# A post-norm residual block on one core: x loaded in three pieces, LayerNorm statistics taken for four row groups at a time, and another route for the last output

## The chip, the core and the metric

The kernel runs on one core of a Trainium2 chip. The metric is the device time of one execution in microseconds. Before the change it is 26.49 us, the median of six runs (26.14 to 26.74). The profile below is of one execution; the span from its first to its last instruction is 24.9 us, some 1.6 us less than the device time, because the device time also holds what comes ahead of the first instruction and after the last.

## The reference

```python
# x: (4, 256, 256) fp32, i.e. 1024 rows of 256; w_block: (256, 256); gamma: (256,)
h = np.maximum(x @ w_block, 0.0)
y = x + h
mu = y.mean(-1, keepdims=True)
sigma = np.sqrt(y.var(-1, keepdims=True) + 1e-6)
return ((y - mu) / sigma * gamma).astype(np.float32)
```

The 1024 rows lie on 128 partitions. A partition holds eight rows, and the kernel works on two of them at once: a "pair" is a tile of 128 partitions x 2 rows x 256 columns, and there are four pairs, numbered 0 to 3 here. Pairs 0 and 1 are the first half of x, pairs 2 and 3 the second. What the changed kernel calls a quad is two pairs, so four row groups.

## The kernel before

Loads first: `w` and `gamma` come over ScalarE's DMA queue in fp32 and are cast to bf16 on chip. x comes over GpSimd's queue, which casts it to bf16 on the way, in two loads of two pairs each.

```python
    w_stage = const.tile([P, KC, D], FP32)
    nc.scalar.dma_start(out=w_stage, in_=w_block.rearrange("(kc p) n -> p kc n", p=P))
    w_sb = const.tile([P, KC, D], BF16)
    nc.scalar.copy(out=w_sb, in_=w_stage)
    # ... gamma_stage in the same way, cast by VectorE; eps_sb; make_identity(nc, ident)
    x_sb = []
    for h in range(NH):                                     # NH = 2
        t_ = xp.tile([P, G, D], BF16, name=f"x_sb{h}", tag=f"x{h}")   # G = 4 rows
        nc.gpsimd.dma_start(out=t_, in_=x_v[h])
        x_sb.append(t_)
```

Then one loop over the four pairs. TensorE transposes x, ScalarE copies the transposed tile out of PSUM, TensorE multiplies by w, ScalarE applies relu, VectorE adds x and takes mean and variance; ScalarE and VectorE make 1/sigma; VectorE normalises; GpSimd multiplies by gamma and writes fp32; SyncE's queue sends the tile out.

```python
    for pr in range(n_pairs):                               # 4 pairs
        # ... 4 transposes of x into pxt (PSUM)
        nc.scalar.copy(out=xt_sb, in_=pxt)                          # L89
        # ... 4 matmuls of xt_sb with w_sb into ph (PSUM)           # L94
        nc.scalar.activation(out=relu_h, in_=ph, func=AF.Relu)      # L103
        nc.vector.tensor_tensor(out=y, in0=x_sb[h][:, f0:f0+PAIR, :], in1=relu_h, op=ALU.add)  # L106
        for t in range(PAIR):
            nc.vector.bn_stats(out=bn6[:, t, :], in_=y[:, t, :])    # L113
            nc.vector.bn_aggr(out=mv[:, t, :], in_=bn6[:, t, :])    # L114
        nc.scalar.activation(out=std, in_=mv[:, :, 1], func=AF.Sqrt, bias=eps_sb)   # L117
        nc.vector.reciprocal(out=rstd, in_=std)                     # L119
        for t in range(PAIR):
            nc.vector.tensor_scalar(tq[:, t, :], in0=y[:, t, :], scalar1=mv[:, t, 0:1],
                scalar2=rstd[:, t:t+1], op0=ALU.subtract, op1=ALU.mult)             # L123
        nc.gpsimd.tensor_tensor(out=o, in0=tq,
            in1=gamma_sb.to_broadcast([P, PAIR, D]), op=ALU.mult)   # L133, fp32 out
        nc.sync.dma_start(out=out_v[h][:, f0:f0+PAIR, :], in_=o)    # L137
```

A scheduler decides in which order the instructions of different pairs stand on an engine, so that order is not the loop's.

Of the kernel before, what the change touches and what calls it, by code (L numbers as in the profile page):

```python
# [1 line left out]

# [6 lines left out]

FP32 = mybir.dt.float32
BF16 = mybir.dt.bfloat16
AF = mybir.ActivationFunctionType
ALU = mybir.AluOpType
AX = mybir.AxisListType


@with_exitstack
def kernel(
    ctx: ExitStack,  # L20
    tc: tile.TileContext,
    x: bass.AP,
    w_block: bass.AP,
    gamma: bass.AP,
    out: bass.AP,
):
    nc = tc.nc
    P = 128

    x_flat = x.flatten_outer_dims()  # L30
    out_flat = out.flatten_outer_dims()
    N, D = x_flat.shape
    assert D == 256 and N == 1024
    KC = D // P
    G = 4
    NH = N // (P * G)
    PAIR = 2
    n_pairs = N // (P * PAIR)

    eps = 1e-6  # L40

    x_v = x_flat.rearrange("(h q f) d -> h q f d", q=P, f=G)
    out_v = out_flat.rearrange("(h q f) d -> h q f d", q=P, f=G)

    const = ctx.enter_context(tc.tile_pool(name="const", bufs=1))
    xp = ctx.enter_context(tc.tile_pool(name="xp", bufs=2))
    xtp = ctx.enter_context(tc.tile_pool(name="xtp", bufs=3))
    hp = ctx.enter_context(tc.tile_pool(name="hp", bufs=3))
    yp = ctx.enter_context(tc.tile_pool(name="yp", bufs=3))
    op_ = ctx.enter_context(tc.tile_pool(name="op", bufs=3))  # L50
    stat = ctx.enter_context(tc.tile_pool(name="stat", bufs=4))
    ps_xt = ctx.enter_context(tc.tile_pool(name="ps_xt", bufs=2, space=bass.MemoryType.PSUM))
    ps_h = ctx.enter_context(tc.tile_pool(name="ps_h", bufs=4, space=bass.MemoryType.PSUM))

    w_stage = const.tile([P, KC, D], FP32)
    nc.scalar.dma_start(out=w_stage, in_=w_block.rearrange("(kc p) n -> p kc n", p=P))
    w_sb = const.tile([P, KC, D], BF16)
    nc.scalar.copy(out=w_sb, in_=w_stage)  # L58

    gamma_stage = const.tile([P, 1, D], FP32)  # L60
    nc.scalar.dma_start(out=gamma_stage, in_=gamma.partition_broadcast(P))
    gamma_sb = const.tile([P, 1, D], BF16)
    nc.vector.tensor_copy(out=gamma_sb, in_=gamma_stage)  # L63

    eps_sb = const.tile([P, 1], FP32)
    nc.vector.memset(eps_sb, eps)

    ident = const.tile([P, P], BF16)
    make_identity(nc, ident)

    x_sb = []
    for h in range(NH):
        t_ = xp.tile([P, G, D], BF16, name=f"x_sb{h}", tag=f"x{h}")
        nc.gpsimd.dma_start(out=t_, in_=x_v[h])  # L74
        x_sb.append(t_)

    for pr in range(n_pairs):
        h = (pr * PAIR) // G
        f0 = (pr * PAIR) % G

        pxt = ps_xt.tile([P, PAIR, KC, P], BF16)
        for t in range(PAIR):
            for c in range(KC):
                nc.tensor.transpose(  # L84
                    pxt[:, t, c, :], x_sb[h][:, f0 + t, ts(c, P)], ident
                )

        xt_sb = xtp.tile([P, PAIR, KC, P], BF16)
        nc.scalar.copy(out=xt_sb, in_=pxt)  # L89

        ph = ps_h.tile([P, PAIR, D], FP32)
        for t in range(PAIR):
            for c in range(KC):
                nc.tensor.matmul(  # L94
                    ph[:, t, :],
                    lhsT=xt_sb[:, t, c, :],
                    rhs=w_sb[:, c, :],
                    start=(c == 0),
                    stop=(c == KC - 1),
                )  # L100

        relu_h = hp.tile([P, PAIR, D], BF16)
        nc.scalar.activation(out=relu_h, in_=ph, func=AF.Relu)  # L103

        y = yp.tile([P, PAIR, D], BF16)
        nc.vector.tensor_tensor(  # L106
            out=y, in0=x_sb[h][:, f0 : f0 + PAIR, :], in1=relu_h, op=ALU.add
        )

        bn6 = stat.tile([P, PAIR, 6], FP32)  # L110
        mv = stat.tile([P, PAIR, 2], FP32)
        for t in range(PAIR):
            nc.vector.bn_stats(out=bn6[:, t, :], in_=y[:, t, :])  # L113
            nc.vector.bn_aggr(out=mv[:, t, :], in_=bn6[:, t, :])  # L114

        std = stat.tile([P, PAIR], FP32)
        nc.scalar.activation(out=std, in_=mv[:, :, 1], func=AF.Sqrt, bias=eps_sb)  # L117
        rstd = stat.tile([P, PAIR], FP32)
        nc.vector.reciprocal(out=rstd, in_=std)  # L119

        tq = op_.tile([P, PAIR, D], BF16)
        for t in range(PAIR):
            nc.vector.tensor_scalar(  # L123
                tq[:, t, :],
                in0=y[:, t, :],
                scalar1=mv[:, t, 0:1],
                scalar2=rstd[:, t : t + 1],
                op0=ALU.subtract,
                op1=ALU.mult,
            )  # L130

        o = op_.tile([P, PAIR, D], FP32, tag="out")
        nc.gpsimd.tensor_tensor(  # L133
            out=o, in0=tq, in1=gamma_sb.to_broadcast([P, PAIR, D]), op=ALU.mult
        )

        nc.sync.dma_start(out=out_v[h][:, f0 : f0 + PAIR, :], in_=o)  # L137


# [1 line left out]
_INS = ['x', 'w_block', 'gamma']  # L141
_OUTS = [((4, 256, 256), 'float32')]


# [23 lines left out]
```

## Time and profile before

| what | value |
| --- | --- |
| device time, median of 6 | 26.49 us (26.14 to 26.74) |
| span of the profiled execution | 24.9 us |
| VectorE (DVE) busy | 9.4 us, 38% of the span |
| ScalarE (ACT) busy | 8.5 us, 34% |
| GpSimd (POOL) busy | 6.6 us, 27% |
| TensorE (PE) busy | 4.9 us, 20% |
| first x load, issue to landing | 6.2 us |
| second x load, issue to landing | 6.4 us |
| an output store of 256 KB, issue to landing | 2.0 us |

No engine is busy for even half of the span, so the shares do not say what bounds the kernel; the order of events does. The table of engine timelines gives, for each instruction or run of equal instructions, when it starts and how long it takes, counted from the first instruction. The chain of waits follows the work that ended last back to what released it. A tile name with a number, such as x_sb_97, is the program's: x_sb_97 is the first x load and x_sb_99 the second.

### The profile page before, as it was taken

The page shows a single profiled execution, that of the slowest core. Times are in us where ns is not written, and L with a number is a line of the kernel's source. Part 1 is how long each engine was busy: PE and PEld are TensorE (multiplying, and loading weights), DVE is VectorE, ACT ScalarE, POOL GpSimd, SP SyncE. Part 2 cuts the span into 40 slices and gives each one's busy share as a digit, 9 for nine tenths or more (in the row PEclk, how much of TensorE's full clock was granted, in tenths as well). Part 3 has the DMA queues.
Part 4 walks back from the last instruction along what each step waited for, and adds up shares of the span by engine and source line. Part 5 has one row for each costly group of instructions (what it writes and reads, how often), then busy time and mean ns, then how long its engine had stood idle before and what let it go on. Part 6 is the DMA issues. An engine that isn't in the chain of part 4 may idle for free.

```text
span 24.9 us, 182 instructions
## 1 busy us (share of the span) xinstructions
PE 4.9 (20%) x32; PEld 3.4 (14%) x32; DVE 9.4 (38%) x34; ACT 8.5 (34%) x15; POOL 6.6 (27%) x12
## 2 busy tenths in 40 slices
PE   0000000000009699995970000000000000000000
PEld 0000000000009267690730000000000000000000
DVE  0000000000400000199960699999998992000000
ACT  0029836000000971789999991000053000000000
POOL 3398500000000000000000029708901975930000
PEclk9999999999999999999999998555555555555555
DMA  0006997999954000000000000007305500822800
GB/s 0 0 13 115 345 72 58 118 140 204 204 102 89 13 0 0 0 0 0 0 0 0 0 0 0 0 0 293 128 0 224 197 0 0 332 89 109 313 0 0
DMA packets 1280, 1.97 MB, mean 79 GB/s; under 512 B 128, under 2 KB 512, under 8 KB 1280
## 3 DMA queue, kind: packets, MB, share of 16 engines
q0 software_dynamic: 288, 0.52, 12.3%
q1 hardware_dynamic: 576, 1.05, 11.2%
q10 hardware_dynamic: 416, 0.39, 10.5%
HBM read 1.44 MB, written 1.05 MB: 100 GB/s over the span
## 4 chain that ended last, share of the span: by engine, by line
DVE 26%; DMA 25%; ACT 12%; PE 10%; issue 7%; POOLq 5%; POOL 1%; DVEq 0%
DMA x_sb_97<-in_x_dram 25%; DVE tq L123 11%; PE ph L94 8%; ACT xt_sb L89 6%; DVE y L106 6%; POOLq L163 5%; ACT L117 3%; DVE bn_181 L113 3%; DVE bn_213 L113 3%; PE pxt L84 2%; ACT relu_h L103 2%; DVE rstd L119 2%; DVE mv L114 2%; ACT std L117 1%; POOL ident masks.py:197 1%
## 5 line engine op out<-in xcount | busy, mean ns | idle before, releaser
L133 POOL TENSOR_TENSOR o<-tq,gamma_sb 128x512 f32<-128x512 bf16 x4 | 4.7, 1176 | 14.4 <-DVE tq L123 12.8
L89 ACT COPY xt_sb<-pxt 128x512 bf16<-128x512 bf16 x4 | 2.1, 590 | 4.0 <-PE pxt L84 4.0
L123 DVE TENSOR_SCALAR tq<-y,mv,rstd 128x256 bf16<-128x256 bf16 x8 | 3.2, 435 | 0.1
L94 PE MATMUL ph<-w_sb,xt_sb 128*128 128x256 bf16 x16 | 3.0, 350 | 0.6 <-ACT xt_sb L89 0.6
L103 ACT ACTIVATE relu_h<-ph 128x512 bf16<-128x512 f32 x4 | 2.3, 590 | 0.9 <-PE ph L94 0.9
L84 PE MATMUL pxt<-ident,x_sb_97 128*128 128x128 bf16 x8 | 1.0, 311 | 7.5 <-DMA x_sb_97<-in_x_dram 7.5
L106 DVE TENSOR_TENSOR y<-x_sb_97,relu_h 128x512 bf16<-128x512 bf16 x2 | 0.8, 410 | 4.0 <-ACT relu_h L103 4.0
L63 DVE CAST gamma_sb<-gamma_stage 128x256 bf16<-128x256 f32 x1 | 0.3, 293 | 5.4 <-DMA gamma_stage<-in_gamma_dram 5.4
L117 ACT ACTIVATE std<-mv,eps_sb 128x2 f32<-128x2 f32 x4 | 1.2, 294 | 3.3 <-DVE mv L114 3.3
L94 PEld LDWEIGHTS <-xt_sb 128*128 128x128 bf16 x16 | 1.7, 121 | 1.6 <-ACT xt_sb L89 1.1
L58 ACT ACT_TABLE_LOAD x1 | 1.3, 1283 | 1.7 <-PEq L152 1.7
L84 PEld LDWEIGHTS <-x_sb_97 128*128 128x128 bf16 x8 | 0.8, 141 | 7.5 <-DMA x_sb_97<-in_x_dram 7.5
L106 DVE TENSOR_TENSOR y<-x_sb_99,relu_h 128x512 bf16<-128x512 bf16 x2 | 1.6, 804 | 0.0
L117 ACT ACT_TABLE_LOAD x1 | 1.3, 1283 | 0.0
L84 PE MATMUL pxt<-ident,x_sb_99 128*128 128x128 bf16 x8 | 1.1, 314 | 0.0
L119 DVE RECIPROCAL rstd<-std 128x2 f32<-128x2 f32 x4 | 0.7, 164 | 1.0 <-ACT std L117 1.0
L84 PEld LDWEIGHTS <-x_sb_99 128*128 128x128 bf16 x8 | 0.9, 151 | 0.1
L74 POOL DMA_DIRECT2D x_sb_97<-in_x_dram x1 | 0.7, 717 | 0.3 <-issue 0.3
L58 ACT CAST w_sb<-w_stage 128x512 bf16<-128x512 f32 x1 | 0.6, 617 | 0.5 <-DMA w_stage<-in_w_block_dram 0.5
L113 DVE BATCH_NORM_STATS2 bn_213<-y 128x6 f32<-128x256 bf16 x2 | 0.8, 390 | 0.0
L113 DVE BATCH_NORM_STATS2 bn_117<-y 128x6 f32<-128x256 bf16 x2 | 0.8, 418 | 0.0
L113 DVE BATCH_NORM_STATS2 bn_149<-y 128x6 f32<-128x256 bf16 x2 | 0.8, 418 | 0.0
(13 smaller groups left out, 3.5 us busy)
## 6 DMA issues: line engine op xcount, KB each, us to landing
out_dram<-o SPq DMA_DIRECT2D x4, 256.0 KB, 2.0
w_stage<-in_w_block_dram ACTq DMA_DIRECT2D x1, 256.0 KB, 2.8
x_sb_97<-in_x_dram POOLq DMA_DIRECT2D x1, 256.0 KB, 6.2
x_sb_99<-in_x_dram POOLq DMA_DIRECT2D x1, 256.0 KB, 6.4
gamma_stage<-in_gamma_dram ACTq DMA_DIRECT2D x1, 128.0 KB, 5.0
```

The lines of the kernel that those rows point to most:

```text
L58: nc.scalar.copy(out=w_sb, in_=w_stage)
L84: nc.tensor.transpose(pxt[:, t, c, :], x_sb[h][:, f0 + t, ts(c, P)], ident)
L89: nc.scalar.copy(out=xt_sb, in_=pxt)
L94: nc.tensor.matmul(ph[:, t, :], lhsT=xt_sb[:, t, c, :], rhs=w_sb[:, c, :], start=(c == 0), stop=(c == KC - 1),)
L103: nc.scalar.activation(out=relu_h, in_=ph, func=AF.Relu)
L106: nc.vector.tensor_tensor(out=y, in0=x_sb[h][:, f0 : f0 + PAIR, :], in1=relu_h, op=ALU.add)
L113: nc.vector.bn_stats(out=bn6[:, t, :], in_=y[:, t, :])
L117: nc.scalar.activation(out=std, in_=mv[:, :, 1], func=AF.Sqrt, bias=eps_sb)
L119: nc.vector.reciprocal(out=rstd, in_=std)
L123: nc.vector.tensor_scalar(tq[:, t, :], in0=y[:, t, :], scalar1=mv[:, t, 0:1], scalar2=rstd[:, t : t + 1], op0=ALU.subtract, op1=ALU.mult,)
L133: nc.gpsimd.tensor_tensor(out=o, in0=tq, in1=gamma_sb.to_broadcast([P, PAIR, D]), op=ALU.mult)
L163: with _tile.TileContext(nc) as tc:
```

## The change

Three things are done, each for a reason that the program text gives.

- x is loaded in three pieces instead of two, pair 0 alone, pair 1 alone, and pairs 2 and 3 together, so that pair 0 need not wait for pair 1's data. The identity and the x loads also stand ahead of the w and gamma loads in the program text.
- The square root and the reciprocal are taken once for two pairs (128x4 values) instead of once for each pair (128x2).
- The last pair's multiplication by gamma moves from GpSimd to VectorE and writes bf16; its store then goes over GpSimd's queue, which casts to fp32 on the way. The other three pairs keep the old route.

```diff
+    x_load_slices = [(0, 0, PAIR), (0, PAIR, G), (1, 0, G)]
+    for li, (h, fs, fe) in enumerate(x_load_slices):
+        t_ = xp.tile([P, fe - fs, D], BF16, name=f"x{li}", tag=f"x{li}")
+        nc.gpsimd.dma_start(out=t_, in_=x_v[h][:, fs:fe, :])
...
-    for h in range(NH):
-        t_ = xp.tile([P, G, D], BF16, name=f"x_sb{h}", tag=f"x{h}")
-        nc.gpsimd.dma_start(out=t_, in_=x_v[h])
...
-    for pr in range(n_pairs):
+    for qd in range(n_pairs // QUAD):
+        ys = []
+        for pq in range(QUAD):
...          (transposes, copy, matmuls, relu, y, bn_stats, bn_aggr as before)
+        nc.scalar.activation(out=std, in_=mv[:, :, 1], func=AF.Sqrt, bias=eps_sb)
+        nc.vector.reciprocal(out=rstd, in_=std)
+        for pq in range(QUAD):
...          (two tensor_scalar for the pair as before)
+            if not last:
+                nc.gpsimd.tensor_tensor(out=o, in0=tq, in1=gamma_sb.to_broadcast([P, PAIR, D]), op=ALU.mult)
+                nc.sync.dma_start(out=out_v[h][:, f0 : f0 + PAIR, :], in_=o)
+            else:
+                ob = op_.tile([P, PAIR, D], BF16, tag="out_bf16")
+                nc.vector.tensor_tensor(out=ob, in0=tq, in1=gamma_sb.to_broadcast([P, PAIR, D]), op=ALU.mult)
+                nc.gpsimd.dma_start(out=out_v[h][:, f0 : f0 + PAIR, :], in_=ob)
```

## The prediction

> **What bounds the kernel now.** I read the chain of waits first. It runs from the first x load through the first pair's TensorE and ScalarE work to VectorE, stays there from 13.9 us, and ends with GpSimd's last product and its store. So I then read each engine's timeline. First the start, in the page's list of costliest groups (engine, output and inputs, count; busy and mean ns; idle time before and what ended it) and its list of transfers:
>
> ```profile
> L84 PE MATMUL pxt<-ident,x_sb_97 128*128 128x128 bf16 x8 | 1.0, 311 | 7.5 <-DMA x_sb_97<-in_x_dram 7.5
> x_sb_97<-in_x_dram POOLq DMA_DIRECT2D x1, 256.0 KB, 6.2
> gamma_stage<-in_gamma_dram ACTq DMA_DIRECT2D x1, 128.0 KB, 5.0
> ```
>
> Nothing computes before 7.49 us. Next ScalarE's timeline (start, us, what):
>
> ```profile
> 9.85 0.60 ACT L103 ACTIVATE relu_h<-ph 128x512 bf16<-128x512 f32 x1 [0.64 <-PE ph L94]
> 10.71 0.60 ACT L103 ACTIVATE relu_h<-ph 128x512 bf16<-128x512 f32 x1 [0.26 <-PE ph L94]
> 11.20 1.07 ACT L89 COPY xt_sb<-pxt 128x512 bf16<-128x512 bf16 x2
> 12.29 1.28 ACT L117 ACT_TABLE_LOAD   x1
> 13.58 0.29 ACT L117 ACTIVATE std<-mv,eps_sb 128x2 f32<-128x2 f32 x1
> ```
>
> The first std ends at 13.88 because ScalarE runs four copies, two relus and a table load before it; VectorE waits 1.03 us for it. After that VectorE never rests for long. Its timeline and GpSimd's, around two places:
>
> ```profile
> 14.80 1.25 POOL L133 TENSOR_TENSOR o<-tq,gamma_sb 128x512 f32<-128x512 bf16 x1 [11.94 <-DVE tq L123]
> 15.15 1.19 DVE L106 TENSOR_TENSOR y<-x_sb_99,relu_h 128x512 bf16<-128x512 bf16 x1
> ...
> 19.23 1.15 POOL L133 TENSOR_TENSOR o<-tq,gamma_sb 128x512 f32<-128x512 bf16 x1 [1.15 <-DVE rstd L119]
> 19.33 1.39 DVE L123 TENSOR_SCALAR tq<-y,mv,rstd 128x256 bf16<-128x256 bf16 x2
> 20.85 1.15 POOL L133 TENSOR_TENSOR o<-tq,gamma_sb 128x512 f32<-128x512 bf16 x1 [0.47 <-POOL o L133]
> ```
>
> An addition that takes 0.42 us elsewhere takes 1.19 here, and ends 0.29 after GpSimd's product (16.05). Two normalisations that take 0.58 take 1.39; the first alone takes 1.13. So GpSimd's product holds VectorE off, twice, for about 0.8 us each. At the end: product 20.85 to 22.00, store issued at 22.0, landed 2.0 us later at 24.0, and 0.9 us of closing work to 24.9. The bound is a chain of latencies: load, ScalarE's six operations and table load, VectorE with two blockings, store.
>
> **What the Trainium skill says.** "SBUF — State Buffer", section "Who interferes with whom": VectorE in a two-port mode, or with two SBUF inputs, and a GpSimd operation that reads SBUF exclude each other for a whole instruction. The trace agrees (1.19 and 1.13 us above); bn_stats, with one input, ran beside GpSimd's second product in its usual 0.39 to 0.42 us. "ScalarE: Activation LUTs", section "What ACT_TABLE_LOAD costs": about 1283 ns; the trace has 1283. "DMA: Bandwidth & Descriptors", section "SWDGE vs HWDGE vs iDMA": a casting transfer must come from GpSimd, where software writes the descriptors. The trace has 0.72 and 0.56 us of GpSimd time for the two x issues, and 0.33 to 0.37 on SyncE's queue for a store.
>
> **Part 1, the x load.** Of the 6.2 us little is x's own: its queue's packets are 12.3% of the span, 3.06 us for both loads, 1.53 each, so 0.77 for one pair. The rest is contention and latency. The DMA row (slices of 0.62 us) gives 345 GB/s in slice 4, which is w, then 72, 58, 118, 140, then 204 twice, which is x alone. Summing the row, 0.54 MB have moved by 5.6 us; w (0.26) and gamma (0.13) are in it, so about 0.14 MB of x, just above one pair (0.13 MB as bf16). Pair 0 could thus have its data at 5.5 to 5.9 us (its packets are half as large and share turns with gamma's). The old load had its 0.26 MB, by the same sum, at about 6.2 and landed at 7.45, 1.25 later, some of that being slow engines. With 0.8 to 1.2 us for the shorter one, pair 0 lands at about **6.65**, a gain of 0.8 (0.3 to 1.1). The split adds one GpSimd issue (0.56) behind it, so pairs 2 and 3 still land near the old 8.7 to 9.2.
>
> **Part 2, ScalarE up to the first std.** The order of instructions in the built program has changed. Before: copy, copy, relu, relu, copy, copy, table load, std. Now: copy 0, relu 0, copies 1 and 2, relus 1 and 2, copy 3, table load, std. One relu more (0.5) stands ahead of the table load, and TensorE now multiplies pair 0 before it transposes pair 1, so copy 1 comes after relu 0. With the durations of the trace: transposes 6.70 to 7.32 (four took 0.62), copy 0 to 7.93, four matmuls to 9.05 (1.05 from 8.78 to 9.83 before), relu 0 to 9.67, copies 1 and 2 to 10.77, matmuls 1 to about 10.95, relu 1 to 11.6, matmuls 2 and relu 2 to 12.3, copy 3 to 12.8, table load to 14.1, std to **14.35**. That is 0.5 us later than the old 13.88: the gain of part 1 is eaten in this order. In exchange VectorE has by then done pair 2's addition and statistics too (0.42 + 0.74), which it did after the first std before.
>
> **Part 3, VectorE from the first std to the last store.** Removed: two of four std (0.29 each, mostly hidden) and two of four reciprocals (0.17 each). Remaining serial work, from the trace's durations: reciprocal and two aggregations 0.25, four normalisations 1.08, addition 0.4, two bn_stats and aggregations 0.95, std with handover 0.35, reciprocal 0.2, four normalisations 1.1, product in bf16 0.43 (as the addition of the same shape): 4.8 us. GpSimd's three products (1.15 each) exclude normalisations and additions. One fits beside bn_stats, aggregation, std and reciprocal (1.5 us in all); the other two hold VectorE off by about 1.1 each. Depending on whether GpSimd gets between two normalisations or only after them, blocking sums to 1.8 to 2.3. So the last bf16 product ends 6.6 to 7.1 us after the first std; with 6.9, at 21.2. The old kernel issued its last store at 22.0.
>
> **Part 4, the last store.** It now costs GpSimd 0.56 to 0.72 us of descriptors, where the old store's data started to move about 0.85 us after its issue. Data: 0.77 us, as for one pair of x. Receipt as before, about 0.4. I take 2.5 us to landing against 2.0, an estimate. So 21.2 + 2.5 = 23.7, and with the same 0.9 of closing a span of 24.6: 0.3 less than 24.9, of which product and store together give about 0.3 (1.28 of GpSimd replaced by 0.43 + 0.08, minus 0.5 for the slower route). Device time 26.49 - 0.3 = 26.2; I leave 0.1 for the third load's extra traffic and say **26.3**.
>
> **Rivals.**
> - ScalarE's order does not cost what I say: TensorE is warm early and std ends by 13.6. For it: the later transposes ran at about 0.13 us each, the first at 0.155. Against: the copies and relus are fixed at 0.59. This would give 25.5.
> - The x load gains nothing, because gamma's slow packets (5.0 us to landing) hold the smaller packets of pair 0 as well. Then std comes at 15.1 and the time is 27.1. For it: 72 and 58 GB/s while the DMA engines are nine and seven tenths busy.
> - GpSimd's store is much slower than 2.5 us. The only such transfers in the trace took 6.2 and 6.4, though in a crowd. At 3.3 us the time is 27.0.
> - GpSimd's product becomes the bound: pairs 0 and 1 are normalised together, so their products queue (2.3 us), and the last store must stand behind the third product on GpSimd. If all three run back to back without gaps it is still 3.5 us after about 15.2, so 18.7, which is before 20.5. It delays by blocking, not by its own length. Unlikely to cost over 0.4.
>
> **Range and chances.** I take errors of about 0.4 us for the x load, 0.4 for the store, 0.5 for the blocking and 0.3 for ScalarE's order; as independent errors they make 0.8 us. Eight in ten is then about 25.3 to 27.2. Two per cent of 26.49 is 0.53, so the borders are 25.96 and 27.02. From 26.3 they lie 0.4 and 0.9 of such an error away: about one third below, a fifth above, the rest between.
>
> **What would show it.** The first transposes at 6.7 (right from 6.4 to 7.2); the first 128x4 std ending near 14.35, behind seven ScalarE operations and the table load; a normalisation or addition of over 1 us beside the first product and another beside the third; the bf16 product at about 0.43; the store landing 2.5 us after issue. I am wrong above all if the first transposes move by under 0.3, if no VectorE operation is held off beside GpSimd, or if the store takes over 3 us.

## The result, and the profile after

The changed kernel takes 25.85 us (median of ten, 25.5 to 26.37), the kernel before 26.51 us in the executions beside it. The ratio is 0.972, with a 95% interval of 0.967 to 0.978: faster by nearly three per cent. The ratios here and below leave out disturbed executions; the medians hold all. The span of the profiled execution is 24.0 us instead of 24.9. The old profile is of an execution of 26.68 us, a little above the median, so spans differ by 0.9 and times by 0.66.

The start first, from the page of the changed kernel: a group of instructions (with what ended the idle time before it), then two transfers with the time from issue to landing in the last column.

```profile
L103 PE MATMUL pxt<-ident,x_87 128*128 128x128 bf16 x4 | 0.6, 308 | 5.3 <-DMA x_87<-in_x_dram 5.3
...
gamma_stage<-in_gamma_dram ACTq DMA_DIRECT2D x1, 128.0 KB, 3.4
x_87<-in_x_dram POOLq DMA_DIRECT2D x1, 128.0 KB, 4.0
```

TensorE starts at 5.30 us, not 7.49: pair 0 is there 2.2 us sooner (other profiles with the old loads have 7.04 to 7.50). Gamma, whose load nobody touched, landed after 3.4 us instead of 5.0. Now ScalarE's timeline up to the first std (start, us, what, idle before it):

```profile
7.66 0.60 ACT L120 ACTIVATE relu_h<-ph 128x512 bf16<-128x512 f32 x1 [1.13 <-PE ph L111]
...
9.86 0.60 ACT L120 ACTIVATE relu_h<-ph 128x512 bf16<-128x512 f32 x1 [0.64 <-PE ph L111]
10.93 0.60 ACT L120 ACTIVATE relu_h<-ph 128x512 bf16<-128x512 f32 x1 [0.47 <-PE ph L111]
11.42 0.58 ACT L106 COPY xt_sb<-pxt 128x512 bf16<-128x512 bf16 x1
12.02 1.28 ACT L131 ACT_TABLE_LOAD   x1
13.31 0.30 ACT L131 ACTIVATE std<-mv,eps_sb 128x4 f32<-128x4 f32 x1
```

The first std ends at 13.61, only 0.27 sooner than the old 13.88. Of the 2.2 us 1.9 are spent again on the way there. Relu 2 now stands ahead of the table load (0.6 us), and the relus ahead of it wait 2.2 us for TensorE in all (the idle times above) instead of 0.9 (0.64 and 0.26 in the old timeline). Next VectorE's timeline from there to the end:

```profile
13.87 1.93 DVE L144 TENSOR_SCALAR tq<-y,mv,rstd 128x256 bf16<-128x256 bf16 x4
15.72 0.41 DVE L123 TENSOR_TENSOR y<-x_91,relu_h 128x512 bf16<-128x512 bf16 x1
16.17 0.75 DVE L128 BATCH_NORM_STATS2 bn_161<-y 128x6 f32<-128x256 bf16 x2
...
17.72 1.95 DVE L144 TENSOR_SCALAR tq<-y,mv,rstd 128x256 bf16<-128x256 bf16 x4
19.70 0.43 DVE L161 TENSOR_TENSOR ob<-tq,gamma_sb 128x512 bf16<-128x512 bf16 x1
```

and GpSimd's:

```profile
14.54 1.18 POOL L155 TENSOR_TENSOR o<-tq,gamma_sb 128x512 f32<-128x512 bf16 x1 [11.19 <-DVE tq L144]
15.88 1.26 POOL L155 TENSOR_TENSOR o<-tq,gamma_sb 128x512 f32<-128x512 bf16 x1 [0.16 <-DVE tq L144]
18.40 1.18 POOL L155 TENSOR_TENSOR o<-tq,gamma_sb 128x512 f32<-128x512 bf16 x1 [1.25 <-DVE tq L144]
20.42 0.60 POOL L164 DMA_DIRECT2D out_dram<-ob  x1 [0.84 <-DVE ob L161]
```

Four normalisations take 1.93 us where two pairs of 0.58 would take some 1.1, and each time a GpSimd product starts in the middle of them. GpSimd's second product, at 15.88, runs beside the addition and the statistics, which take their usual time. The last product ends at 20.13, the casting store begins at 20.42, lands 2.3 later at 22.7, and the span ends at 24.0.

So the 0.9 us of span come from these differences. The first std is 0.27 sooner. From the end of that std to the end of the last product there are 6.52 us instead of 8.12 (13.88 to 22.00): 1.6 less, above all because pair 2's addition and statistics (0.42 + 0.74) are already done and because the last product takes 0.43 instead of 1.15. Handover and store cost 2.6 us instead of 2.0, and the closing, from the last landing to the end of the span, 1.3 instead of 0.9: one microsecond given back.

The identity and the x loads also moved up in the program text. The issues did not move with them: the first x load is issued at 1.25 us and w's at 0.74 in both profiles.

### The profile page after: what moved, and what is told of

Its sections match the earlier page's. It is cut to its first block, busy times and chain, and to the rows that moved or that the text cites. A ratio compares the mean times of both kernels' runs of the same rounds, so it can differ in the third digit from the quotient of the medians.

```text
span 24.0 us, 180 instructions
## 1 busy us (share of the span) xinstructions
PE 5.8 (24%) x32; PEld 3.7 (15%) x32; DVE 10.1 (42%) x33; ACT 8.1 (34%) x13; POOL 6.6 (28%) x13
## 4 chain that ended last, share of the span: by engine, by line
ACT 18%; DVE 17%; DMA 17%; PE 16%; issue 9%; POOL 6%; POOLq 3%
DMA x_87<-in_x_dram 17%; PE ph L111 12%; DVE tq L144 10%; ACT xt_sb L106 7%; POOL o L155 5%; ACT L131 5%; PE pxt L103 3%; ACT relu_h L120 3%; DVE bn_161 L128 3%; POOLq L190 3%; ACT std L131 3%; DVE rstd L132 2%; DVE mv L129 2%; DVE y L123 1%; POOL ident masks.py:197 1%
## 5 line engine op out<-in xcount | busy, mean ns | idle before, releaser
L155 POOL TENSOR_TENSOR o<-tq,gamma_sb 128x512 f32<-128x512 bf16 x3 | 3.6, 1208 | 12.6 <-DVE tq L144 12.6
L111 PE MATMUL ph<-w_sb,xt_sb 128*128 128x256 bf16 x16 | 4.2, 416 | 1.9 <-ACT xt_sb L106 1.9
L144 DVE TENSOR_SCALAR tq<-y,mv,rstd 128x256 bf16<-128x256 bf16 x8 | 3.9, 549 | 0.0
L123 DVE TENSOR_TENSOR y<-x_87,relu_h 128x512 bf16<-128x512 bf16 x1 | 0.4, 426 | 3.4 <-ACT relu_h L120 3.4
L131 ACT ACTIVATE std<-mv,eps_sb 128x4 f32<-128x4 f32 x2 | 0.6, 298 | 3.1 <-DVE mv L129 3.1
L128 DVE BATCH_NORM_STATS2 bn_103<-y 128x6 f32<-128x256 bf16 x4 | 1.5, 418 | 0.1
L128 DVE BATCH_NORM_STATS2 bn_161<-y 128x6 f32<-128x256 bf16 x4 | 1.5, 418 | 0.0
L164 POOL DMA_DIRECT2D out_dram<-ob x1 | 0.6, 602 | 0.8 <-DVE ob L161 0.8
L123 DVE TENSOR_TENSOR y<-x_91,relu_h 128x512 bf16<-128x512 bf16 x2 | 0.8, 402 | 0.0
```

The costliest lines, as they stand in the source:

```text
L111: nc.tensor.matmul(ph[:, t, :], lhsT=xt_sb[:, t, c, :], rhs=w_sb[:, c, :], start=(c == 0), stop=(c == KC - 1),)
L123: nc.vector.tensor_tensor(out=y, in0=xs, in1=relu_h, op=ALU.add)
L128: nc.vector.bn_stats(out=bn6[:, g, :], in_=y[:, t, :])
L155: nc.gpsimd.tensor_tensor(out=o, in0=tq, in1=gamma_sb.to_broadcast([P, PAIR, D]), op=ALU.mult)
```

## The experiments

**Each part alone, and all but the split.**

The split alone, on the old kernel:

```diff
-    for h in range(NH):
-        t_ = xp.tile([P, G, D], BF16, ...); nc.gpsimd.dma_start(out=t_, in_=x_v[h])
+    for li, (h, fs, fe) in enumerate([(0, 0, PAIR), (0, PAIR, G), (1, 0, G)]):
+        t_ = xp.tile([P, fe - fs, D], BF16, ...); nc.gpsimd.dma_start(out=t_, in_=x_v[h][:, fs:fe, :])
...          (x_pairs names the tile and rows of each pair)
```

> The old kernel with the load of x in three pieces and nothing else. Theory A: the smaller first load lands near 5.3 us, as in the changed kernel, and in the order that results two copies, one relu fewer stand ahead of the first std than in the changed kernel (copy 0, relu 0, copies 1 and 2, relu 1, table load, std), so the first std ends near 12 us instead of 13.88 and the time falls by 1 to 1.8 us, to about 25. Rival B: the early landing in the changed kernel's profile was chance of that execution (gamma, which was not changed, also landed 1.6 us sooner), so the first load lands near 6.65 and the time is 25.8 to 26.3.

Measured: 26.01 us against 26.42, ratio 0.981 (0.975 to 0.988). The first transposes begin at 5.38, so the early landing was no chance. ScalarE's and VectorE's timelines in this run:

```profile
10.55 1.28 ACT L118 ACT_TABLE_LOAD   x1
11.85 0.30 ACT L118 ACTIVATE std<-mv,eps_sb 128x2 f32<-128x2 f32 x1
...
12.26 0.41 DVE L114 BATCH_NORM_STATS2 bn<-y 128x6 f32<-128x256 bf16 x1
...
13.18 0.39 DVE L114 BATCH_NORM_STATS2 bn<-y 128x6 f32<-128x256 bf16 x1
...
19.16 0.17 DVE L120 RECIPROCAL rstd<-std 128x2 f32<-128x2 f32 x1 [0.36 <-ACT std L118]
```

The first std ends at 12.15, as theory A said, 1.7 us sooner than in the old kernel. But the time fell by 0.4, not by 1 to 1.8. My step from "first std" to "end" was wrong: VectorE still has pair 1's two bn_stats to take after the std (0.41 and 0.39), which it used to take before it, and it waits 0.36 us for the last std. Here the earlier std only exchanges waiting on VectorE before it for work after it.

The tail alone, on the old kernel:

```diff
+        if pr == n_pairs - 1:
+            nc.vector.tensor_tensor(out=ob, in0=tq, in1=gamma..., op=ALU.mult)     # ob is bf16
+            nc.gpsimd.dma_start(out=out_v[h][:, f0 : f0 + PAIR, :], in_=ob)
+        else: ...  # product on GpSimd in fp32, store from SyncE's queue, as before
```

> The old kernel with only the last pair's product on VectorE in bf16 and its store over GpSimd's queue. Theory A: the product ends 0.85 us sooner (0.43 instead of 1.28), but the store starts 0.3 after it, takes 2.3 instead of 2.0 and the closing is 0.4 longer, so the net is nothing: 26.3 to 26.7. Rival B: the shorter tail is what made the changed kernel faster, and this has 25.8.

Measured: 26.61 against 26.42, ratio 1.009 (1.006 to 1.012). Theory A holds, at its unfavourable end: the new tail by itself loses a little. GpSimd's timeline and a line of the list of transfers:

```profile
21.31 0.60 POOL L143 DMA_DIRECT2D out_dram<-ob  x1 [1.09 <-DVE ob L140]
...
out_dram<-ob POOLq DMA_DIRECT2D x1, 256.0 KB, 2.4
```

The product ended at 21.01, the store begins 0.3 later, lands at 23.7, and the span ends at 24.9: a closing of 1.2.

The statistics for two pairs alone, made from the changed kernel by undoing the split and the tail:

```diff
-    x_load_slices = [(0, 0, PAIR), (0, PAIR, G), (1, 0, G)]
+    x_load_slices = [(0, 0, G), (1, 0, G)]
...          (x_pair finds each pair in the two tiles)
-            last = pr == n_pairs - 1
+            last = False
```

> The old kernel with only the statistics taken for two pairs at a time (two x loads, all products on GpSimd, all stores on SyncE's queue). All four relus now stand ahead of the table load and the first std, so that ends near 15 us instead of 13.88; VectorE has then done all additions and statistics, and eight normalisations and four GpSimd products remain, which exclude each other: 8 x 0.28 + 4 x 1.2 = 7 us, to 22.3, against 22.0. Theory A: same or slower, 26.5 to 27.1. Rival B: fewer std and reciprocals save over 0.5 us, 25.9.

Measured: 27.23 against 26.42, ratio 1.024 (1.015 to 1.032). ScalarE shows why:

```profile
12.03 1.09 ACT L115 ACTIVATE relu_h<-ph 128x512 bf16<-128x512 f32 x2 [0.21 <-PE ph L106]
13.13 1.28 ACT L126 ACT_TABLE_LOAD   x1
14.43 0.30 ACT L126 ACTIVATE std<-mv,eps_sb 128x4 f32<-128x4 f32 x1
```

Relus 2 and 3 moved ahead of the table load, and the first std ends at 14.73 although x landed 0.45 sooner than in the old kernel's profile. Batching the statistics alone is a loss, a little above theory A's 26.5 to 27.1.

The changed kernel with the old two loads of x:

```diff
-    x_load_slices = [(0, 0, PAIR), (0, PAIR, G), (1, 0, G)]
+    x_load_slices = [(0, 0, G), (1, 0, G)]
...          (x_pair finds each pair in the two tiles)
```

> The changed kernel with the old two loads of x. Theory A (the split carries the gain, through the early landing and through the order it lets the scheduler choose): the first std waits for all four relus and ends near 15 us, 8 x 0.28 + 3 x 1.2 + 0.43 = 6.3 us later the last product, then 0.3 + 2.3 + 1.3: span 25.5, time about 27, slower than both kernels. Rival B: the split does little, and this is within 0.3 us of the changed kernel's 25.85.

Measured: 27.64, ratio 1.038 (1.029 to 1.047), slower as theory A said, by 0.6 more than its 27. The first std and VectorE's last product:

```profile
14.89 0.30 ACT L126 ACTIVATE std<-mv,eps_sb 128x4 f32<-128x4 f32 x1
...
21.59 0.43 DVE L156 TENSOR_TENSOR ob<-tq,gamma_sb 128x512 bf16<-128x512 bf16 x1
```

Without the split the changed kernel is slower than the old one. Taking the parts alone, they would change the time by -0.4, +0.2 and +0.8 us; together they change it by -0.66. They do not add: on the batched form the split takes off 1.8 us (27.64 to 25.85), on the old form 0.4. On the batched form it moves the first std from 15.19 to 13.61, partly because one relu fewer stands ahead of it (0.6), and the end of the last product by 1.9, from 22.02 to 20.13. On the old form the first std moved by 1.7 and the end of the last product by 0.7 (21.32 against 22.00).

**The tail, within the changed kernel.**

```diff
-            last = pr == n_pairs - 1
+            last = False        # GpSimd's fp32 product and SyncE's store for all pairs
```

> The changed kernel with the last pair's product back on GpSimd in fp32 and its store back on SyncE's queue; split and statistics for two pairs stay. Theory A (the new tail gains nothing, as in the old kernel): the third product ended at 19.58, the fourth then runs 19.8 to 20.95, store landed 22.95, closing 0.9: span 23.85 against 24.0, time 25.5 to 25.9. Rival B: beside the earlier start the shorter tail does carry part of the gain, and this has 26.1 or more.

Measured: 25.74, ratio to the old kernel 0.973 (0.964 to 0.983); the changed kernel has 0.972. So the new tail contributes nothing here either. GpSimd's last two products:

```profile
18.50 1.19 POOL L155 TENSOR_TENSOR o<-tq,gamma_sb 128x512 f32<-128x512 bf16 x1 [1.26 <-DVE tq L144]
19.90 1.15 POOL L155 TENSOR_TENSOR o<-tq,gamma_sb 128x512 f32<-128x512 bf16 x1 [0.22 <-POOL o L155]
```

The last one ends at 21.05, 0.9 later than VectorE's product in the changed kernel; the plain store and the shorter closing return it. This also compares split and statistics together (0.973) with the split alone (0.981, 0.975 to 0.988): with the split, batching costs nothing, and may gain a little; the intervals overlap.

The new tail with a plain store:

```diff
-                ob = op_.tile([P, PAIR, D], BF16, tag="out_bf16")
+                ob = op_.tile([P, PAIR, D], FP32, tag="out_last")
-                nc.gpsimd.dma_start(out=..., in_=ob)
+                nc.sync.dma_start(out=..., in_=ob)
```

> The changed kernel, but VectorE writes the last product in fp32 and SyncE's queue stores it, so no casting store over GpSimd. Theory A: the product takes about 0.6 us instead of 0.43, the store starts at once, lands in 2.0 and the closing is 0.9 as in the old kernel: 20.3 + 2.05 + 0.9 = 23.25, time about 25.1. Rival B: the closing after the last landing is longer for another reason than the GpSimd store (GpSimd being idle late, say), and this has 25.5 or more.

Measured: 25.03, ratio 0.951 (0.945 to 0.956), as theory A said. VectorE's timeline, and SyncE's:

```profile
19.61 0.69 DVE L161 TENSOR_TENSOR ob<-tq,gamma_sb 128x512 f32<-128x512 bf16 x1
...
20.33 0.33 SPq L164 DMA_DIRECT2D out_dram<-ob  x1
```

The product takes 0.69 instead of 0.43, the store begins 0.03 after it, lands in 2.0 to 2.1, and the closing is 0.8. So the shorter tail pays with a plain store and not with the casting one.

**The first std.**

```diff
+    nc.vector.memset(eps_sb, eps)
+    nc.scalar.activation(out=warm, in_=eps_sb, func=AF.Sqrt, bias=eps_sb)   # warm: 128x1, not used
     nc.scalar.copy(out=w_sb, in_=w_stage)
```

> The changed kernel with one square root of a single column ahead of the first copy, so that the square root's table is loaded at the start, while ScalarE waits for w, and no second table load stands ahead of the first std. Theory A (the first std sets when VectorE can normalise): std ends near 12.3 instead of 13.6, VectorE starts normalising at about 13.1 instead of 13.87, because it still has pair 2's statistics to take; time 25.0 to 25.3. Rival B: VectorE's own work or GpSimd's products set the end, and the time stays above 25.6.

Measured: 24.94, ratio 0.947 (0.942 to 0.953). ScalarE's timeline:

```profile
10.89 0.58 ACT L108 COPY xt_sb<-pxt 128x512 bf16<-128x512 bf16 x1
12.20 0.30 ACT L133 ACTIVATE std<-mv,eps_sb 128x4 f32<-128x4 f32 x1 [0.73 <-DVE mv L131]
```

No table load stands between them any more, std waits for VectorE's statistics and ends at 12.50, and normalising starts at 13.00 instead of 13.87. The table load was on the path, and what came after it moved up as a whole. The result of the extra square root isn't used. The casts of w and gamma stand behind it in the program text; the loads are issued when they were (w 0.74, gamma 1.19, x 1.27 us).

Both edits together:

> Both of the last two edits together on the changed kernel. Theory A: the two gains lie at different places of one chain and add: about 24.4. Rival B: one hides the other, and it is no better than the better of the two alone.

Measured: 24.26, ratio 0.920 (0.913 to 0.927). Alone they take 0.91 and 0.82 us off the changed kernel's 25.85; together 1.59 of the 1.73: they nearly add.

**GpSimd's products.** In place of the normalisation and GpSimd's product, on the last version:

```diff
+                nc.vector.scalar_tensor_tensor(out=tq[:, t, :], in0=y[:, t, :], scalar=mv[:, g, 0:1],
+                    in1=gamma_sb[:, 0, :], op0=ALU.subtract, op1=ALU.mult)
+                nc.scalar.activation(out=o[:, t, :], in_=tq[:, t, :], func=AF.Copy, scale=rstd[:, g:g+1])
...
+            nc.sync.dma_start(out=out_v[h][:, f0 : f0 + PAIR, :], in_=o)      # all pairs
```

> The version with the square root's table first and the last store from SyncE's queue (24.26 us), with GpSimd's products gone altogether: VectorE takes (y - mean) x gamma in one instruction per row group, ScalarE scales by 1/sigma and writes fp32, SyncE's queue stores all pairs. Theory A (VectorE's two long normalisations, of 1.2 us beside GpSimd's products, are exclusion): no VectorE instruction takes over 0.8 us, ScalarE's eight scalings of 0.4 to 0.5 set the end near 18.1, time about 22.9. Rival B (those instructions are slow for another reason, or ScalarE becomes a worse bound): 24.0 or more.

Measured: 23.57, ratio 0.882 (0.873 to 0.892). The last lines of VectorE's and ScalarE's timelines:

```profile
16.19 0.84 DVE L147 SCALAR_TENSOR_TENSOR tq<-y,mv,gamma_sb 128x256 bf16<-128x256 bf16 x2
...
17.16 1.70 ACT L155 ACTIVATE o<-tq,rstd 128x256 f32<-128x256 bf16 x4 [0.56 <-DVE rstd L134]
```

Two of VectorE's new instructions together take 0.84 to 0.87, none comes near the 1.17 of a blocked one, all additions take 0.41 to 0.43, and ScalarE's four scalings end at 18.86 (18.1 was expected). The gain is 0.7 us, where I expected 1.4: each new instruction takes 0.45 to 0.48 against 0.33 to 0.34 for the plain normalisation, so part of what the blocking cost is paid in another form. That the long instructions vanish together with GpSimd's work fits exclusion, and so do the overlaps in the earlier traces; the experiment changes the form of the instructions too, so it does not prove it alone.

**Why x lands sooner.** In eight profiles with a small first load the first transposes begin between 5.21 and 5.42 us; in the four with the plain two loads between 7.04 and 7.50. To see whether the length of the runs does it, the old loads with a padded tile, so that the loads are cut into runs of 2 KB in the source:

```diff
-        t_ = xp.tile([P, G, D], BF16, ...)
+        t_ = xp.tile([P, G // PAIR, PAIR + 1, D], BF16, ...)       # the row behind each pair isn't used
-        nc.gpsimd.dma_start(out=t_, in_=x_v[h])
+        nc.gpsimd.dma_start(out=t_[:, :, 0:PAIR, :], in_=x_v[h].rearrange("q (a b) d -> q a b d", b=PAIR))
```

> The old kernel with its two loads of x, but each row of the tile is padded behind every pair, so that a load's contiguous runs in the source are 2 KB instead of 4 KB, as in the small loads of the changed kernel. Amount of data, number of transfers and order of all instructions stay. Theory A (the length of the runs decides how x, w and gamma share the DMA engines): gamma lands about 3.3 us after its issue instead of 4.5 to 5.0, the first x load (still two pairs) near 6.2 instead of 7.0 to 7.5, time 25.2 to 25.7. Rival B (the early landing comes from waiting for half as much data): gamma and the first x land as in the old kernel, time 26.2 to 26.6.

Measured: 26.32 (ratio 0.980, 0.976 to 0.985), and on its list of transfers

```profile
x_sb<-in_x_dram POOLq DMA_DIRECT2D x2, 256.0 KB, 6.0
...
gamma_stage<-in_gamma_dram ACTq DMA_DIRECT2D x1, 128.0 KB, 4.0
```

Gamma lands sooner (4.0 against 4.5 to 5.0), but x does not: the transposes begin at 7.23. Theory A falls as the explanation for x. Why this run is two per cent faster than the old kernel stays open.

Gamma out of the way of the old loads:

```diff
-    nc.scalar.dma_start(out=gamma_stage, in_=gamma.partition_broadcast(P))
+    nc.gpsimd.dma_start(out=gamma_stage, in_=gamma.partition_broadcast(P))   # behind both x loads
```

> The old kernel with gamma's load issued behind both x loads on GpSimd's queue, so that its 128 short reads no longer run beside the first x load. Theory A (gamma's slow reads hold x): the first x load lands near 6.0, time about 25.2. Rival B (x is slow by itself or beside w): it lands at 7.0 or later and the time is 26 or more.

Measured: 25.51 (24.14 to 25.93, four executions, which scatter too much for a ratio) against 26.55. The first transposes in the profiled one (25.39 us):

```profile
6.16 1.03 PE L84 MATMUL pxt<-ident,x_sb 128*128 128x128 bf16 x8 [6.16 <-DMA x_sb<-in_x_dram]
```

They begin 0.9 to 1.3 us sooner than with gamma beside. Theory A holds for the old load: gamma's load delays it by about 1 us, and the time falls by about as much. The last run is the same edit on the version without GpSimd's products, where the first load is small:

> The version without GpSimd products (23.57 us) with gamma's load issued behind the three x loads on GpSimd's queue. In the old kernel this edit let the first x load land 1.1 to 1.3 us sooner. Theory A (gamma's reads still hold the small first load): it lands near 4.7 instead of 5.3 us, time 22.9 to 23.3. Rival B (with the small first load gamma no longer matters for it, only for the loads behind it): the first load lands at 5.1 to 5.4 and the time stays within 0.2 of 23.57.

Measured: 23.9 (22.93 to 24.23, six executions, again no ratio). The first transposes:

```profile
5.42 0.61 PE L105 MATMUL pxt<-ident,x 128*128 128x128 bf16 x4 [5.42 <-DMA x<-in_x_dram]
```

They begin at 5.42 against 5.38 with gamma beside, as rival B said; the median time, 0.3 above 23.57, fits neither theory. This profile is of the slowest of the six executions, and there is none of the one that took 22.93, so it is not shown that gamma never matters for the small load. As far as these profiles go, the split's gain has two terms: freedom from gamma, 0.9 to 1.3 us (7.04 to 7.50 against 6.16), and half the data, 0.7 (6.16 against 5.42). Why gamma delays a large first load and not a small one is open; gamma's own landing moves too, from 4.5 to 5.0 us beside large loads to 3.1 to 3.5 beside small ones.

## Why the prediction came out as it did

The time was 26.3 predicted, with a range of 25.3 to 27.2, and is 25.85. The prediction gave nearly half to a change within two per cent and one chance in three to a larger gain, which came true. The mechanism was right in part: the order on ScalarE eats most of the early start, and GpSimd's products hold VectorE off twice. But the prediction took its whole gain of 0.3 us from the tail and none from the split with the batched statistics. The runs have it the other way round: the tail gives nothing, and the other two parts together, with the old tail, give 0.7 (25.74 against 26.45). By steps:

- **Part 1, the x load.** 6.65 was predicted for the landing, 5.25 measured; the gain of 0.8 was 2.2 and outside its own band of 0.3 to 1.1. The failed term is the sum over the DMA row: it took the old row, in which gamma and a large load slow each other, as the supply of the new one. With gamma moved, the old load came about 1 us sooner and the small one, in its one profile, no sooner. Pairs 2 and 3 landed at 7.5 us (issued at 2.82, 4.7 later), not near 8.7 to 9.2.
- **Part 2, ScalarE to the first std.** The order was read rightly, and so was its meaning, that it eats the gain. From the first transposes to the end of std I had 7.65 us; it was 8.31. The term that was too small is the second and third groups of four matmuls, some 0.7 each or less in my sum and 1.04 and 1.06 in the trace, so relu 2 ended 6.2 instead of 5.6 after the start. (Lines of both runs stand below.) The Trainium skill, "TensorE: Matmul & The Clock Gate", section "Part 1: The HAM clock gate", has the array at half rate until it has been busy for a free-running window of some 3.4 us. The traces agree in kind: all groups stayed slow in the changed kernel (mean 416 ns), and with the same order they sped up at the third group in the run with the square root's table first (mean 344 ns). That this gate is the cause is not shown: the mean granted clock of the changed kernel's profile reads 1.0. The landing came 1.4 us sooner than predicted and this stretch took 0.66 longer, so the two errors partly cancelled.
- **Part 3, VectorE.** From std to the last product I had 6.6 to 7.1 and took 6.9; it was 6.52. Two blockings were predicted, with 1.8 to 2.3 us in all; there are two, of 0.85 each (1.93 and 1.95 less 1.08 to 1.1), not 1.1 each, so 1.7 in all. The rest is 4.8, as in my sum. One product did fit beside the statistics, without holding anything off.
- **Part 4, the store.** 2.5 us from product to landing, measured 2.6. The closing after the landing was taken as the old 0.9 and is 1.3 (1.2 in the run with the tail alone, 0.8 with SyncE's store). With that term the tail's gain of 0.3 is gone, as two runs show (26.61 against 26.42 on the old kernel, 25.85 against 25.74 on the changed one).
- **The rivals.** ScalarE's order did cost what I said and more. The rival that gamma would hold the small load as long as the large one is refuted: with gamma beside it, its transposes began at 5.21 to 5.42 us in seven profiles. The store was not much slower. GpSimd's product blocked and did not bound.

The second and third groups of matmuls in the changed kernel, and the third in the run with the square root's table first, where TensorE's order is the same:

```profile
8.79 1.04 PE L111 MATMUL ph<-w_sb,xt_sb 128*128 128x256 bf16 x4 [0.31 <-ACT xt_sb L106]
9.83 1.06 PE L111 MATMUL ph<-w_sb,xt_sb 128*128 128x256 bf16 x4
...
9.76 0.60 PE L113 MATMUL ph<-w_sb,xt_sb 128*128 128x256 bf16 x4
```

So the net was near partly by luck: the x load's gain was underrated by 1.4 us, slower matmuls and the closing took back 1.1, and VectorE's section gave 0.4 more.

## What to carry to other kernels

A part of a change is worth what it moves at the end, not where it acts: here the split moved the start by some 2 us, and the time by 0.4 on the old kernel and by 1.8 beside the batched statistics. Batching lost 0.8 alone and nothing beside the split: what stood ahead of the table load in ScalarE's order differed. Ask of every early gain which instruction stands in front of the next one in that engine's order. And where a tail is cut by moving a product to a faster engine, see what its store costs: here writing fp32 with a plain store was 0.8 us faster than bf16 with a casting one.

## What the runs showed of the hardware that was not expected

- A store from GpSimd's queue as the last transfer is followed by 1.2 to 1.3 us of closing, one from SyncE's queue by 0.8 to 0.9. Why is open.
- Gamma's load of 128 KB, the same 1 KB for each partition, takes 3.1 to 5.0 us to land, longer than the 256 KB of w (2.7 to 2.9), and delayed a large x load beside it by about 1 us.
- With one square root at the start, ScalarE's copies, relus and square roots ran with a single table load of 1.28 us instead of two; the time fell by 0.9 us.
